# State times w_in in 64x32 TensorE tiles, state reads in column pairs, another split of the vector work, and another order of the first loads

## The chip, the cores and the metric

The kernel runs on one core of one Trainium2 chip. A core has TensorE (PE) for matmuls, VectorE (DVE), ScalarE (ACT) and GpSimd (POOL) for elementwise work, and SyncE (SP), which here only issues DMAs. The metric is the device time of one execution in microseconds, lower is better. The kernel before takes 754.55 us (median of three runs, 753.77 to 754.71).

## What is computed

```python
def _attn_ref(x, state):                       # x 4x8x512x64, state 4x8x32x64
    scores = scale * np.matmul(x, state.transpose(0, 1, 3, 2))
    ...
    xread = np.matmul(a, state)                # a: softmax over the 32 states
    scores2 = scale * np.matmul(state, x.transpose(0, 1, 3, 2))
    ...
    sread = np.matmul(a2, x)                   # a2: softmax over the 512 tokens
    return np.concatenate([xread, sread], axis=2)

def _moe_ref(x, w_in, w_out):                  # 2304 tokens, 512 -> 2048 -> 512
    h = x @ w_in
    g = np.where(h >= 1, h, np.where(h <= -1, 0.0, (h + 1) ** 2 / 4))
    return g @ w_out

def _moe2_ref(x, w_a, w_b, w_out):             # 512 -> 1536 -> 512
    return ((x @ w_a) * (x @ w_b)) @ w_out
```

Attention between 512 tokens and 32 state slots per head (32 heads, 64 wide) gives 2304 rows of 512 numbers, which then pass through two feed-forward blocks. The weights arrive as 8-byte floats and are converted on the chip.

## The kernel before

**The stages.** Phase one, up to the first matmul of 368 columns, does the attention and the first product `h = x @ w_in` with its gate. The rest (`b_chunk`, `ab_run`, `o_run`) does the other three products, by Strassen-like sums of seven, each product in three matmuls of high and low halves; the change leaves it as it is.

**Phase one.** Heads are taken four at a time, in eight "quads" `k`; two quads make one batch of 512 tokens. The tokens' rows of `h` don't need `xread` itself: since `xread = a @ state`, `h` is the sum over heads of `a @ (state @ w_in)`. So `w_state` multiplies the states by the rows of `w_in` that belong to their heads (plain f32, 64 head dimensions contracted, 32 slots a head), for one batch and one group `n` of four of the sixteen 128-wide blocks `f` of `w_in`; the result leaves its bank as a high half (ACT, `hi_of`) and a low half (DVE). `h_mm(j, f)` then multiplies it by the attention weights `att` of batch `j` (six matmuls of 512 columns), 64 such units in all. `a_qk` makes the scores, `a_soft` the softmax over slots and `att`, `s_soft` the softmax over tokens, `s_tr` transposes it on PE, `s_read` multiplies it by the tokens, and `h_state` makes the `h` rows of the states from that (128 matmul records). The blocks of `w_in` and, later, of `w_out` (`vraw`) are converted by `conv`: a DMA into a staging slot, a byte copy (L389 on DVE for `w_in`, on ACT for the others), an ACT copy that rounds (L321), and a DVE operation that puts the word together (L395). Before, `w_state` runs per quad: two matmuls of 64 weight columns with 128 rows, of which half are zeros, side by side in the array.

**The gate** of a unit, four PSUM banks in turn: ACT reads the bank (L613), ACT or POOL squares (L620, L622), DVE combines it with the bank (L627) and so frees it; the result is stored to DRAM (`g_d`). There are 68 gates: 16 for each batch `j` of tokens, and four for the state rows (after the 48th).

**The order.** `Flow` records each operation with the engines that may run it, a cost and its dependencies, and `order()` places them one by one; that fixes each engine's instruction list and, where a choice of engines was given, the engine. An engine runs its list strictly in order. All DMAs are issued by SP, in order, and an issue waits for what was in its slot.

Of the kernel before, what the change touches and what calls it, by code (L numbers as in the profile page):

```python
# [19 lines left out]
class Flow:  # L20
# [48 lines left out]
    def order(self):  # L69
# [24 lines left out]
        for i in range(n - 1, -1, -1):  # L94
# [70 lines left out]
def attention_then_two_mlps(  # L165
# [31 lines left out]
    STEPS = (0, 5, 10, 16, 22, 28, 34, 40)  # L197

# [102 lines left out]
    def t_ts(n):  # L301
        return 0.16 + n * 0.00052
# [55 lines left out]
    def conv(src, k, stage, z, dst=None, by="ACT"):  # L358
# [27 lines left out]
        if by == "ACT":  # L386
            act(to, of, n, AF.Copy, regs(place), regs(z), saturate=False)
        else:
            op({"DVE": t_tt(n)}, lambda e: nc.vector.tensor_copy(to(U8), of(U8)), regs(place), regs(z))  # L389
        act(to, z, n, AF.Copy, regs(z), regs(z), saturate=False)  # L390
# [27 lines left out]
    stage_a = Ring([V("F0", 8256 * i, 2050) for i in range(2)])  # L418
    z_a = Ring([V("F0", 16512 + 4096 * i, 1024) for i in range(1)])
# [9 lines left out]
    def w_in(f, k):  # L429
        conv(w1_k[0, f : f + k], k, stage_a(), z_a(), win.sub(512 * f, 512 * k), by="DVE")  # L430

    def aset(i):
# [9 lines left out]
        {**sets[k % 2], "st": V("FS", 32768 + 1024 * (k % 4), 256), "sm": V("FS", 69632 + 256 * (k % 4), 64)}  # L442
# [9 lines left out]
    def st_load(b):  # L452
        v = V("FS", 32768 + 2048 * (b % 2), 512)
# [3 lines left out]
                out=v().rearrange("p (k n) -> p k n", k=2), in_=st_d[2 * b : 2 * b + 2].rearrange("k p n -> p k n")  # L457
# [3 lines left out]
            1 << 18,  # L461
# [8 lines left out]
    def a_qk(k):  # L470
# [19 lines left out]
    def a_soft(k):  # L490
# [22 lines left out]
        split(*att[k], d["at"])  # L513

    def w_state(b, q, n):
        d = qs[2 * b + q]
        ab = abank()

        def emit(e):
            for p in range(2):  # L520
                r = slice(64 * p, 64 * p + 64)
                c = (2 * q + p) * P
                w = win()[:, 2048 * n : 2048 * (n + 1)].rearrange("p (f x) -> p f x", x=512)[:, :, c : c + P]
                nc.tensor.matmul(  # L524
                    banks[ab][r, :].rearrange("p (f x) -> p f x", x=P), d["st"]()[:, r], w, start=True, stop=True
                )

        op({"PE": 1.05}, emit, regs(d["st"], win.sub(2048 * n, 2048)), [bank(ab)])
        hi, lo = wsum[n][q]
        src = lambda: banks[ab]  # L530
        hi_of(hi, src, 512, [bank(ab)], regs(hi))
        tt(lo, src, lambda: hi(F32), ALU.subtract, 512, [bank(ab)] + regs(hi), regs(lo))

    def s_soft(k):
# [45 lines left out]
    def s_read(k):  # L580
# [756 lines left out]
```

## Time and profile before

| | us |
|---|---|
| median of three runs | 754.55 |
| the profiled execution | 753.63 |
| its span, first to last instruction | 751.9 |
| PE busy | 721.4 |
| DVE busy | 562.6 |
| ACT busy | 433.2 |
| POOL busy | 76.4 |

The profile takes one execution apart. Busy time is the union of an engine's instructions; the rest is waiting. PE is nearly always busy after 62 us, so the others' totals say little by themselves: what counts is, stage by stage, whether PE waits, and for what. The time outside the span is 1.73 us in the profiled execution.

### The profile page before, as it was taken

What the parts mean: (1) busy time and instruction counts of PE and PEld (TensorE: products, weight loads), DVE (VectorE), ACT (ScalarE), POOL (GpSimd) and SP (SyncE); (2) the same over time, 40 slices, a digit from 0 to 9 for tenths busy, and PEclk for the clock granted to TensorE, in tenths of its full rate; (3) what the DMA queues carried; (4) which work ended last, traced back from release to release, by engine and by line L of the source; (5) the groups of instructions that cost most, each with busy time, mean ns of one, the idle gap of its engine ahead of it and who ended that gap; (6) DMA issues with size and microseconds to landing.
All of it is one profiled execution on the core that took longest, in us unless ns stands there. A gap on an engine that the chain in (4) does not pass through costs nothing.

```text
span 751.9 us, 11651 instructions
## 1 busy us (share of the span) xinstructions
PE 721.4 (96%) x4454; PEld 663.6 (88%) x4454; DVE 562.6 (75%) x790; ACT 433.2 (58%) x656; POOL 76.4 (10%) x67
## 2 busy tenths in 40 slices
PE   4898999998999999999999999999999999999997
PEld 2455676685899999999999999999999999999997
DVE  5798887848889668789999966566645699977660
ACT  2687899848644444566556766555433455544440
POOL 2223464318100000000000000000000000000000
PEclk7899999999999999999999999999999999999999
DMA  9776777427756514626134666546452249444211
GB/s 335 252 266 213 256 259 267 168 93 247 253 189 189 169 41 148 208 69 193 63 118 146 209 238 211 188 137 221 136 168 79 83 129 292 135 141 127 86 43 43
DMA packets 75513, 127.92 MB, mean 170 GB/s; under 512 B 5696, under 2 KB 50240, under 8 KB 75456
## 3 DMA queue, kind: packets, MB, share of 16 engines
q1 hardware_dynamic: 75456, 127.16, 51.4%
q8 instruction: 35, 0.57, 0.3%
q14 instruction: 22, 0.18, 0.1%
HBM read 83.89 MB, written 43.25 MB: 169 GB/s over the span
## 4 chain that ended last, share of the span: by engine, by line
PE 81%; DMA 6%; DVE 6%; ACT 2%; POOL 2%; issue 2%; SPq 0%; DVEq 0%; ACTq 0%; POOLq 0%
PE bank L345 74%; DMA f<-in_w_dram 3%; PE bank L524 2%; PE bank L658 2%; ACT f L321 2%; POOL f L622 1%; DMA fs<-in_st_dram 1%; PE bank L478 1%; DVE r L330 1%; DMA p_d<-f 1%; DVE f L627 1%; PE bank L589 1%; DMA f<-p_d 1%; DVE rh L330 1%; DVE fs L395 1%
## 5 line engine op out<-in xcount | busy, mean ns | idle before, releaser
L345 PE MATMUL bank<-rh,r 128*128 128x352 f32 (+2 forms) x1398 | 222.2, 316 | 2.1 <-DVE f L330 0.9
L345 PEld LDWEIGHTS bank<-rh,r 128*128 128x128 f32 x1398 | 215.7, 189 | 3.0 <-DVE f L330 1.2
L321 ACT ACTIVATE f<-bank 128x368 f32<-128x368 f32 (+3 forms) x183 | 82.8, 455 | 142.1 <-PE bank L345 141.7
L345 PE MATMUL bank<-r,r 128*128 128x368 f32 (+1 forms) x960 | 157.5, 316 | 0.0
L345 PEld LDWEIGHTS bank<-r,r 128*128 128x128 f32 x960 | 148.7, 189 | 0.5 <-DVE r L330 0.5
L321 ACT ACTIVATE rh<-f 128x736 fp32r<-128x736 f32 (+5 forms) x120 | 100.7, 845 | 78.9 <-PE bank L345 69.5
L330 DVE TENSOR_TENSOR rh<-f,rh 128x736 fp32r<-128x736 f32 (+5 forms) x120 | 116.1, 972 | 36.3 <-ACT rh L321 33.6
L330 DVE TENSOR_TENSOR f<-bank,f 128x368 f32<-128x368 f32 (+2 forms) x168 | 85.4, 516 | 76.1 <-PE bank L345 65.9
L345 PE MATMUL bank<-r 128*128 128x512 f32 (+1 forms) x582 | 123.1, 363 | 4.1 <-DVE f L627 4.0
L345 PEld LDWEIGHTS bank<-r 128*128 128x128 f32 x582 | 95.0, 191 | 34.0 <-DVE f L627 7.9
L330 DVE TENSOR_TENSOR f<-f 128x256 f32<-128x256 f32 (+7 forms) x142 | 116.8, 842 | 2.9 <-DMA f<-p_d 2.4
L330 DVE TENSOR_TENSOR r<-f,r 128x768 fp32r<-128x768 f32 (+5 forms) x88 | 94.3, 1079 | 18.1 <-ACT r L321 17.7
L321 ACT ACTIVATE r<-f 128x768 fp32r<-128x768 f32 (+5 forms) x88 | 80.7, 924 | 32.2 <-PE bank L345 22.9
L321 ACT ACTIVATE f<-f 128x1024 fp8e5<-128x1024 f32 (+1 forms) x77 | 85.6, 1111 | 17.7 <-DVE f L395 6.3
L345 PE MATMUL bank<-rh 128*128 128x352 f32 (+2 forms) x564 | 93.1, 318 | 0.0
L345 PEld LDWEIGHTS bank<-rh 128*128 128x128 f32 x564 | 88.4, 189 | 0.6 <-DVE f L330 0.6
L345 PE MATMUL bank<-r,rh 128*128 128x368 f32 (+1 forms) x480 | 81.0, 316 | 0.0
L345 PEld LDWEIGHTS bank<-r,rh 128*128 128x128 f32 x480 | 74.7, 189 | 0.2 <-DVE rh L330 0.2
L524 PE MATMUL bank<-fs 128*64 128x512 f32 x128 | 33.1, 632 | 14.5 <-DVE fs L395 12.2
L622 POOL TENSOR_TENSOR f<-f 128x512 f32<-128x512 f32 x25 | 34.1, 1376 | 61.6 <-ACT f L613 61.5
L395 DVE SCALAR_TENSOR_TENSOR f<-f 128x1024 uint32<-128x1024 uint32 (+1 forms) x34 | 33.1, 973 | 6.0 <-ACT f L321 5.9
L627 DVE SCALAR_TENSOR_TENSOR f<-f,bank 128x512 f32<-128x512 f32 x40 | 26.8, 678 | 13.0 <-ACT f L620 6.7
(50 smaller groups left out, 376.7 us busy)
## 6 DMA issues: line engine op xcount, KB each, us to landing
f<-in_w_dram SPq DMA_DIRECT2D x25, 1024.0 KB, 5.4
f<-p_d SPq DMA_DIRECT2D x17, 768.0 KB, 5.3
f<-g_d SPq DMA_DIRECT2D x32, 368.0 KB, 4.6
g_d<-f SPq DMA_DIRECT2D x40, 256.0 KB, 2.7
f<-in_w_dram SPq DMA_DIRECT2D x18, 512.0 KB, 3.9
p_d<-f SPq DMA_DIRECT2D x48, 184.0 KB, 2.1
g_d<-fs SPq DMA_DIRECT2D x28, 256.0 KB, 2.6
f<-g_d SPq DMA_DIRECT2D x16, 352.0 KB, 3.8
```

Of the source, the lines that this page charges most:

```text
L321: lambda e: nc.scalar.activation(dst(), src(), func, **{k: (v() if callable(v) else v) for k, v in kws.items()}),
L330: op({"DVE": t_tt(n)}, lambda e: nc.vector.tensor_tensor(dst(), a(), b(), alu), rd, wr)
L345: nc.tensor.matmul(o, w, x, start=first and k == 0, stop=last and k == n - 1, skip_group_check=onto)
L395: lambda e: nc.vector.scalar_tensor_tensor(out(U32), words_of(1, U32)(), 5, z(U32), ALU.logical_shift_right, ALU.bitwise_or),
L478: nc.tensor.matmul(banks[b][r, :], d["st"]()[:, r], d["xld"]()[:, p * 512 : (p + 1) * 512], start=True, stop=True)
L524: nc.tensor.matmul(banks[ab][r, :].rearrange("p (f x) -> p f x", x=P), d["st"]()[:, r], w, start=True, stop=True)
L589: nc.tensor.matmul(banks[ab][:, p * 64 : (p + 1) * 64], d["xn"]()[:, c * 256 + p * 128 : c * 256 + (p + 1) * 128], d["a2t"]()[:, c * 128 + ...
L622: nc.gpsimd.tensor_tensor(g(), g(), g(), ALU.mult)
L627: lambda e: nc.vector.scalar_tensor_tensor(g(), g(), 1.0, h(), ALU.min, ALU.max),
L658: nc.tensor.matmul(banks[b][:, P * i : P * i + P], w[:, P * c : P * c + P], xs()[:, P * c : P * c + P], start=c == 0, stop=c == 3,)
```

## The change

`w_state` takes both quads of a batch in one operation: eight matmuls of 64 rows by 32 weight columns in place of four of 128 by 64. The zero padding is gone, so the loads of the states halve. The placement alternates: head `j` of quad `q` reads partitions `64*(j%2)`, and writes partitions `32*(j ^ q)` of the bank of its quad. `a_qk` is done in the same kind of tile (four matmuls in one bank). `s_read` uses 16 matmuls of 64 weight columns and 32 moving columns in place of 8 of 128 and 64, and its result leaves in one ACT copy instead of two. In `conv`, the byte copy may go to DVE or POOL (`w_in`) or ACT or POOL (`vraw`); the low half of `att`, the Strassen sums of `vraw` may go to POOL too, and the square of a gate to DVE. `w_in` gets five staging slots and two scratch buffers instead of two and one. The first loads are the tokens of quads 0 and 1, then the states, then five blocks of `w_in`; the token loads for `s_read` of quads 0 and 1 wait for the planner's first `w_state`. `s_tr` and `s_read` come some units after `s_soft`.

```diff
-    def conv(src, k, stage, z, dst=None, by="ACT"):
+    def conv(src, k, stage, z, dst=None, by=("ACT",)):
...
+        t = 0.18 + 0.00116 * n
+        op({x: {"A": t, "D": t_ts(n), "P": 0.2 + 0.0014 * n}[x[0]] for x in by}, copy, regs(place), regs(z))
...
+    stage_w = Ring([V("F0", o, 2050) for o in (0, 8256, 28160, 36416, 44672)])
+    z_w = Ring([V("F0", o, 1024) for o in (16512, 52928)])
...
-        conv(w1_k[0, f : f + k], k, stage_a(), z_a(), win.sub(512 * f, 512 * k), by="DVE")
+        conv(w1_k[0, f : f + k], k, stage_w(), z_w(), win.sub(512 * f, 512 * k), by=("DVE", "POOL") if f else ("DVE", "ACT"))
...
-            for p in range(2):
-                r = slice(64 * p, 64 * p + 64)
+            for j in range(4):
+                r, o, x = slice(64 * (j % 2), 64 * (j % 2) + 64), NS * (j ^ (k % 2)), 512 * (j // 2)
                 nc.tensor.matmul(
-                    banks[b][r, :], d["st"]()[:, r], d["xld"]()[:, p * 512 : (p + 1) * 512], start=True, stop=True
+                    banks[b][o : o + NS, :],
+                    d["st"]()[r, NS * j : NS * j + NS],
+                    d["xld"]()[r, x : x + 512],
...
-        split(*att[k], d["at"])
...
+        op(
+            {"DVE": t_tt(512), "POOL": 1.3},
+            lambda e: eng(e).tensor_tensor(lo(), d["at"](), hi(F32), ALU.subtract),
...
+    def w_state(b, n, f0=0, f1=4):
+        st = [qs[2 * b + q]["st"] for q in range(2)]
+        ab = [abank() for _ in range(2)]
...
+            for j in range(4):
+                for q in range(2):
+                    h, c, o = j % 2, 2 * q + j // 2, NS * (j ^ q)
+                    w = win()[64 * h : 64 * h + 64, 2048 * n + 512 * f0 : 2048 * n + 512 * f1]
+                    nc.tensor.matmul(
+                        banks[ab[q]][o : o + NS, :cols].rearrange("p (f x) -> p f x", x=P),
+                        st[q]()[64 * h : 64 * h + 64, NS * j : NS * j + NS],
+                        w.rearrange("p (f x) -> p f x", x=512)[:, :, c * P : c * P + P],
...
+        flow.gate = first_w[0] if k < 2 else None
         load(d["xn"], lambda: xn_d[k], (), 1 << 19)
...
+                    for e2 in range(2):
+                        nc.tensor.matmul(
+                            banks[ab][64 * e2 : 64 * e2 + 64, p * NS : (p + 1) * NS],
+                            d["xn"]()[:, c * 256 + p * 128 + e2 * 64 : c * 256 + p * 128 + (e2 + 1) * 64],
...
-        op({"ACT": t_act(512), "POOL": 1.1}, square, regs(g), regs(g))
+        op({"ACT": t_act(512), "DVE": t_tt(512), "POOL": 1.3}, square, regs(g), regs(g))
...
-    def v_sum(dst, a, b, alu):
-        tt(dst, a, b, alu, words(dst), regs(a, b), regs(dst))
+    def v_sum(dst, a, b, alu, engs=("DVE",)):
...
+        st_load(0)
         a_load(0)
-        st_load(0)
+        flow.rush = 8.0
         a_load(1)
-        w_in(0, 1)
-        w_in(1, 1)
+        flow.rush = 0.0
+        w_in(0, 2)
         warm(WARM)
         a_part(0)
+        a_part(1)
         w_in(2, 2)
-        w_part(0, 0)
-        a_part(1)
-        w_part(0, 1)
+        first_w.append(len(flow.ops))
+        w_state(0, 0, 0, 2)
+        w_state(0, 0, 2, 4)
```

On SP, from the first issue on, the loads stand like this before (`in_xt` and `in_xn` are the tokens in two layouts, `in_st` the states, `in_w` the weights; 128x4096 is one block of `w_in`, 128x2x4096 two):

```order
L369 DMA f_66<-in_w_dram 128x4096 x2
L309 DMA fs<-in_xt_dram 128x512 x2
L456 DMA fs<-in_st_dram 128x2x256
L309 DMA fs<-in_xt_dram 128x512 x2
L309 DMA fs<-in_xn_dram 128x1024
L456 DMA fs<-in_st_dram 128x2x256
L309 DMA fs<-in_xn_dram 128x1024
L369 DMA f_66<-in_w_dram 128x2x4096 x2
L309 DMA fs<-in_xt_dram 128x512 x4
```

and like this now:

```order
L314 DMA fs<-in_xt_dram 128x512 x4
L468 DMA fs<-in_st_dram 128x2x128
L374 DMA f_66<-in_w_dram 128x2x4096 x5
L468 DMA fs<-in_st_dram 128x2x128
L314 DMA fs<-in_xt_dram 128x512 x4
L374 DMA f_66<-in_w_dram 128x2x4096
L314 DMA fs<-in_xn_dram 128x1024 x2
L374 DMA f_66<-in_w_dram 128x2x4096 x2
```

The tokens and states of the first two quads have moved ahead of all weights, five double blocks of `w_in` follow without a gap, and the `in_xn` loads stand behind six of the eight.

On POOL, the list after the first two quads' softmax was this before (L498 and L508 are `a_soft`, L622 squares of gates):

```order
L498 TENSOR_TENSOR fs<-fs 128x512 x2
L508 TENSOR_TENSOR fs<-fs 128x512 x2
L622 TENSOR_TENSOR f_66<-f_66 128x512 x2
L498 TENSOR_TENSOR fs<-fs 128x512 x2
L622 TENSOR_TENSOR fs<-fs 128x512 x2
L508 TENSOR_TENSOR fs<-fs 128x512 x2
```

and is this now (L514 and L524 are `a_soft`, L396 byte copies of `conv`, L533 low halves of `att`, L651 squares):

```order
L514 TENSOR_TENSOR fs<-fs 128x512 x2
L524 TENSOR_TENSOR fs<-fs 128x512 x2
L396 COPY f_66<-f_66 128x1024
L533 TENSOR_TENSOR r_65<-fs,r_65 128x512 x2
L396 COPY f_66<-f_66 128x1024
L651 TENSOR_TENSOR f_66<-f_66 128x512 x2
L651 TENSOR_TENSOR fs<-fs 128x512 x3
L396 COPY f_66<-f_66 128x1024
```

Byte copies and low halves stand between the softmax steps and the squares now; over the whole program POOL has nine byte copies, four low halves and five sums of 128x4x256 that it didn't have, and three squares fewer (42 for 45).

## Rows read from the trace of the kernel before

**Rows 1.** Busy time by stage: stretch, length, engines' busy us, granted clock, DMA share, GB/s.
```profile
0.00:78.10 78.10, 59.60 (x268) 35.05 (x269) 60.06 (x112) 50.02 (x84) 23.11 (x26) 0.89 0.76 269
78.10:156.30 78.20, 75.91 (x379) 51.96 (x378) 63.46 (x94) 68.96 (x107) 34.45 (x28) 1.00 0.66 226
156.30:198.30 42.00, 37.90 (x211) 31.14 (x211) 27.62 (x32) 27.49 (x38) 18.75 (x13) 0.96 0.64 213
198.30:751.90 553.60, 547.95 (x3601) 545.46 (x3600) 411.42 (x555) 286.74 (x428) 0.05 (x1) 1.00 0.45 145
```

**Rows 2.** PE's waits, longest in total first: total us, times, longest us.
```profile
PE bank L524 <- DVE fs L395: 12.2, 4, 9.3
...
PE bank L345 <- DVE f L627: 4.0, 3, 3.4
```

**Rows 3.** PE in order of time: start us, us, records; idle time before in brackets.
```profile
21.94 3.46 PE L524 MATMUL bank<-fs 128*64 128x512 f32 x8 [9.28 <-DVE fs L395]
...
26.18 3.06 PE L345 MATMUL bank<-r 128*128 128x512 f32 x12
...
75.88 1.94 PE L524 MATMUL bank<-fs 128*64 128x512 f32 x8
...
82.56 1.08 PE L478 MATMUL bank<-fs 128*64 128x512 f32 x4
83.57 2.00 PE L589 MATMUL bank<-fs 128*128 128x64 f32 x16
...
198.34 8.21 PE L345 MATMUL bank<-rh,r 128*128 128x368 f32 x48
```

**Rows 4.** DVE in order of time: the 16th and the 48th gate.
```profile
77.45 0.65 DVE L627 SCALAR_TENSOR_TENSOR f<-f,bank 128x512 f32<-128x512 f32 x1
...
155.62 0.67 DVE L627 SCALAR_TENSOR_TENSOR fs<-fs,bank 128x512 f32<-128x512 f32 x1
```

**Rows 5.** Groups by line and shape in 0 to 198.3 us: busy us, mean ns.
```profile
L622 POOL TENSOR_TENSOR f<-f 128x512 f32<-128x512 f32 x25 | 34.1, 1376 | 61.6 <-ACT f L613 61.5
...
L589 PEld LDWEIGHTS bank<-fs 128*128 128x128 f32 x128 | 15.2, 191 | 3.8 <-ACT fs L321 2.7 <-ACT fs L547 0.8
...
L321 ACT ACTIVATE f<-f 128x1024 fp8e5<-128x1024 fp8e5 x8 | 11.0, 1373 | 0.9 <-DMA f<-in_w_dram 0.9
...
L330 DVE TENSOR_TENSOR f<-f 128x1024 f32<-128x1024 f32 x8 | 10.0, 1252 | 0.0
...
L620 ACT ACTIVATE f<-f 128x512 f32<-128x512 f32 x14 | 8.8, 628 | 0.3
...
L524 PEld LDWEIGHTS bank<-fs 128*64 128x64 f32 x128 | 7.8, 140 | 31.8 <-DVE fs L395 15.0 <-issue 10.1 <-ACT fs L321 4.9
L330 DVE TENSOR_TENSOR r<-fs,r 128x512 fp32r<-128x512 f32 x8 | 6.6, 826 | 0.0
...
L389 DVE COPY f<-f 128x1024 uint8<-128x1024 uint8 x7 | 5.3, 756 | 2.5 <-DMA f<-in_w_dram 2.5
```

**Rows 6.** Busy time by stretch: the head, and the state rows' product.
```profile
0.00:9.00 9.00, 4.26 (x24) 4.10 (x24) 3.27 (x6) 2.82 (x3) 0.70 (x6) 0.94 0.77 257
...
155.00:169.00 14.00, 14.00 (x128) 14.00 (x127) 4.56 (x7) 4.24 (x7) 0.00 (x0) 1.00 0.29 96
```

**Rows 7.** The first scores on PE, in order of time.
```profile
8.97 3.68 PE L478 MATMUL bank<-fs 128*64 128x512 f32 x8 [3.38 <-DMA fs<-in_st_dram]
```

**Rows 8.** A piece of the chain that ended last: start us, us, what.
```profile
46.94 7.80 DMA f<-in_w_dram
```

**Rows 9.** DVE in order of time: the same operation twice.
```profile
110.15 2.05 DVE L330 TENSOR_TENSOR r<-f,r 128x1024 fp32r<-128x1024 f32 x1
...
125.55 1.21 DVE L330 TENSOR_TENSOR r<-f,r 128x1024 fp32r<-128x1024 f32 x1
```

**Rows 10.** POOL in order of time: two products of 512 columns.
```profile
102.41 1.04 POOL L622 TENSOR_TENSOR fs<-fs 128x512 f32<-128x512 f32 x1 [1.54 <-ACT fs L613]
...
111.08 2.02 POOL L508 TENSOR_TENSOR fs<-fs 128x512 f32<-128x512 f32 x1
```

More of the change, by code (lines that the diff above doesn't have):

```diff
@@ L101, in order @@
                 late[i] = min(late[i], ideal[i])
+        late = [x - self.hurry[i] for i, x in enumerate(late)]
         free = dict.fromkeys(self.LAT, 0.0)
@@ L385, in conv, with copy @@
         to, of = lambda dt=F8: byte(z, 4)(dt)[:, :, 3], lambda dt=F8: byte(place.sub(2, 2 * n), 8)(dt)[:, :, 0]
[L386 to L390, printed above, removed]
+        def copy(e):
+            if e == "ACT":
+                nc.scalar.activation(to(), of(), AF.Copy, saturate=False)
+            else:
+                eng(e).tensor_copy(to(U8), of(U8))
+        t = 0.18 + 0.00116 * n
+        op({x: {"A": t, "D": t_ts(n), "P": 0.2 + 0.0014 * n}[x[0]] for x in by}, copy, regs(place), regs(z))
+        act(to, z, n, AF.Copy, regs(z), regs(z), t=t, saturate=False)
         out = words_of(1) if dst is None else dst
@@ L460, in st_load @@
             regs(v),
-            1 << 18,
+            1 << 17,
         )
@@ L512, in a_soft @@
         op({"DVE": 0.71}, lambda e: nc.vector.transpose(d["at"](), t1()), regs(t1), regs(d["at"]))
-        split(*att[k], d["at"])
-    def w_state(b, q, n):
-        d = qs[2 * b + q]
-        ab = abank()
-        def emit(e):
[L520 to L532, printed above, removed]
+        hi, lo = att[k]
@@ new lines, in a_soft @@
+        hi_of(hi, d["at"], 512, regs(d["at"]), regs(hi))
+        op(
+            {"DVE": t_tt(512), "POOL": 1.3},
+            lambda e: eng(e).tensor_tensor(lo(), d["at"](), hi(F32), ALU.subtract),
+            regs(d["at"], hi),
+            regs(lo),
+        )
+    def w_state(b, n, f0=0, f1=4):
+        st = [qs[2 * b + q]["st"] for q in range(2)]
+        ab = [abank() for _ in range(2)]
+        cols = P * (f1 - f0)
+        def emit(e):
+            for j in range(4):
[6 more added lines that the diff above has]
+                        w.rearrange("p (f x) -> p f x", x=512)[:, :, c * P : c * P + P],
+                        start=True,
+                        stop=True,
+                    )
+        op({"PE": 0.3 + cols * 0.0018}, emit, regs(*st, win.sub(2048 * n + 512 * f0, 512 * (f1 - f0))), [bank(b) for b in ab])
+        for q in range(2):
+            hi, lo = (v.sub(P * f0, cols) for v in wsum[n][q])
+            src = lambda q=q: banks[ab[q]][:, :cols]
+            hi_of(hi, src, cols, [bank(ab[q])], regs(hi))
+            tt(lo, src, lambda hi=hi: hi(F32), ALU.subtract, cols, [bank(ab[q])] + regs(hi), regs(lo))
@@ L565, in s_soft @@
         )
+        flow.gate = first_w[0] if k < 2 else None
         load(d["xn"], lambda: xn_d[k], (), 1 << 19)
+        flow.gate = None
     def s_tr(k):
@@ L648, in h_mm @@
         g = (qring if 16 * j + f < SWITCH else qlast)()
-        gate(b, g, lambda: store(lambda: g_d[f, :, S * j : S * j + S], g, [dram("G", f, S * j, S * j + S)], 1 << 18))
+        here = [dram("G", f, S * j, S * j + S)]
+        gate(b, g, lambda: store(lambda: g_d[f, :, S * j : S * j + S], g, here, 1 << 18))
     def h_state(n):
@@ L727, in v_split @@
         tt(rows(lo), src, rows(hi, F32), ALU.subtract, n, regs(src, hi), regs(lo))
-    def v_sum(dst, a, b, alu):
-        tt(dst, a, b, alu, words(dst), regs(a, b), regs(dst))
+    def v_sum(dst, a, b, alu, engs=("DVE",)):
+        n = words(dst)
+        op(
+            {x: t_tt(n) if x == "DVE" else 0.2 + 0.0021 * n for x in engs},
+            lambda e: eng(e).tensor_tensor(dst(), a(), b(), alu),
+            regs(a, b),
+            regs(dst),
+        )
     parts = ((0, 4), (4, 8))
+    BOTH = ("DVE", "POOL")
     def v_early():
@@ L1129, in phase_one @@
     def phase_one():
-        zero(z_a())
+        for _ in range(2):
+            zero(z_w())
         def a_part(k):
@@ L1167, in phase_one @@
                 s_soft(k)
-                s_tr(k)
-                s_read(k)
                 if k + 2 < NQ:
@@ L1174, in phase_one @@
                     a_part(k + 2)
+            if t in READS:
+                k = READS.index(t)
+                s_tr(k)
+                s_read(k)
             if 12 <= t < 44 and t % 4 == 0:
                 flow.gate = units[-1]
-                conv(w1_k[1, nv : nv + 2], 2, stage_a(), z_a(), V("F0", vraw[nv].at, 1024))
+                conv(w1_k[1, nv : nv + 2], 2, stage_a(), z_a(), V("F0", vraw[nv].at, 1024), ("ACT", "POOL"))
                 flow.gate = None
```

52 lines of the change are left out of this document (24 added, 28 removed).

## The prediction

> **What bounds the kernel now.** I first read the busy time stretch by stretch [rows 1], cut at events that the changed kernel has too: the end of the 16th gate on DVE (78.10 us), of the 48th (156.30) [rows 4], and the first matmul of 368 columns (198.34) [rows 3]. Call the stages A, B and C; the last 553.6 us lie behind them. There PE is busy 547.95 of 553.6 us and the change adds no matmul, so I leave that part as it is. In B PE is busy 75.91 of 78.2 us (97%), ACT 68.96 (88%), DVE 63.46 (81%), POOL only 34.45 (44%): PE sets the pace, ACT is close behind, POOL has room. In A PE is busy 59.60 of 78.1, DVE 60.06, ACT 50.02, so no engine fills it. The list of waits says why [rows 2]: `w_state` waited 12.2 us for the converted `w_in`, 9.28 of them before its first matmul at 21.94 us [rows 3]. A later load still stands on the last chain, issued at 46.94 us and 7.8 us long [rows 8]. C has 4.1 us without PE work; gates that DVE took late cost 4.0 in all, nearly all of it there [rows 2].
>
> **PE's work.** One `w_state` for a batch and a group was two pairs of matmuls, 1.94 us for eight records [rows 3]. It is now eight smaller matmuls, sixteen records. No row has a tile of 64 rows by 32 columns. If all eight run at once, the price is that of one pair, 1.94/2 = 0.97 us; if they find no more room than before, 1.94. I take 1.2: `s_read`'s records, 64 moving columns behind a load of 128 weight columns, follow each other at 2.00/16 = 0.125 us [rows 3], a quarter of that for 32 columns is 0.03, and eight more records make 0.97 + 0.24. Sixteen such steps exist, eight in B: 8 x 0.74 = 5.9 us less there.
>
> `s_read` goes from 16 records to 32, with half the weight columns. A load of 64 columns is 191 - 140 = 51 ns shorter than one of 128 [rows 5]. One after another the 32 cost 32 x 0.0625 = 2.0 us, no gain; two columns of the array at once, 1.0. I take 1.3, somewhat under the middle, since the two matmuls of a pair now write separate columns of the array, as `w_state`'s pairs do, whose four records of 512 columns take 0.97. Five of the eight are in B: 5 x 0.7 = 3.5 us. `a_qk` had two tiles at once and has four; I leave it at 1.08.
>
> So PE in B: 75.91 - 5.9 - 3.5 = 66.5 us.
>
> **DVE and ACT in B**, by counting both lists between the 16th and the 48th gate. DVE loses five sums (1.25 each [rows 5]), two low halves of `att` (0.83), two splits of 1024 (1.5, between the two of rows 9) and one word operation (about 1.25), and gets five squares (about 0.63, half a sum) and one more `a_soft` and `s_soft` share that slides over from A (about 4): -6.3 - 1.7 - 3.0 - 1.2 + 3.1 + 4.0 = -5.1, so 58.4 us. ACT loses eight byte copies (1.37), three squares (0.63), two splits (about 1.05), gets some 2 of softmax: 68.96 - 11.0 - 1.9 - 2.1 + 2.0 = 56.0. POOL takes what left: of the nine copies, four low halves and five sums most fall here. A copy on POOL has no row: 0.76 if it runs as on DVE [rows 5], 2.75 if it costs two products of 512 (1.38 each, the mean); I take 1.6. A sum is two products, 2.1 by the short row to 4.0 by the long one [rows 10]; I take 2.75. POOL goes to about 58 us.
>
> PE stays the longest. At the same 97% B takes 68.5 us. With POOL at over 80% squares wait longer in its queue, and behind each the gate on DVE and the bank that PE needs; I add 2. **B: 70.5, 7.7 us less.** Ends: 66.6 (PE without a gap, 1.0 a step) and 74.
>
> **Stage A.** The first scores waited for the states until 8.97 us [rows 7], queued behind 1.57 MB; now they stand behind 1.05. At the head's 257 GB/s [rows 6] that is 2.0 us. The first `w_state` needs one double block instead of two single and one double, and its staging slot waits for nothing. That block ends 2.2 MB into the queue, 8.6 us, and the states landed 1.8 us behind such a count (1.83 MB, 7.1 us): 10.4. Then come on ACT and DVE a byte copy 1.37, a softmax step 0.63, a second copy 1.37 and the word, about 1.25 (a sum of the same size) [rows 5], together 4.6, and a us for what stands between them: the first `w_state` at 16 us instead of 21.94, the first unit, behind the high and low halves, near 21.5 instead of 26.18. The last block of `w_in` stands 11.3 MB into the queue; if the DMA engines don't rest, 269/0.76 = 354 GB/s [rows 1], it lands at 34 us instead of 54.7 [rows 8], so loads leave the chain.
>
> What is left is DVE. Its list up to the 16th gate loses three copies of 1024 and two of 512 (3.2 us), two low halves (1.7), two softmax steps and a half that slide into B (about 4), and gets a memset (0.9) and a square (0.6): 60.06 - 7.4, say 53. Before, DVE was busy 3.27 us until 9.0 [rows 6] and 56.8 of the 69.1 us after, 82%. Now 51 us of work (53 less the memsets) begin at 7. At 82% the gate comes at 69, at 95% at 61. I take 67, nearer to the first, because the chain copy, ACT, word, product, high half, low half still passes between engines for each group. PE has about 40 us of work from 16 on and fits. **A: 67, 11.1 us less.** Ends: 61 and 71.
>
> **Stage C.** DVE gets two splits and one word from B and four squares, about 6.7 us, ACT about 4. During the state rows' product DVE and ACT are busy only 4.56 and 4.24 of 14 us [rows 6], and that hides them; without this cover they would cost up to 6. Of the five sums on POOL two or three now stand before squares. **C: 42.5, 0.5 more.** Ends: 40 (the late gates vanish) and 45.
>
> Sum: 753.63 - 11.1 - 7.7 + 0.5 = 735.3 for an execution like the profiled one; the median of the runs lies 0.92 above that, so **736**.
>
> **Shared paths.** POOL and DVE get in each other's way already: the same split took DVE 2.05 us beside POOL work and 1.21 without [rows 9], a product took POOL 2.02 in the same microseconds and 1.04 alone [rows 10]. In B, two-input DVE work on SBUF falls from about 26 to 18 us while POOL's rises from 34 to 58, so the product of the two, the chance to meet, stays about the same; I add nothing beyond the 2 us above. The Trainium skill (SBUF — State Buffer, on the engine side of the ports) says that a DVE operation with two SBUF inputs and a GpSimd operation exclude each other for a whole instruction. The rows agree; by that rule every move to GpSimd is paid partly by DVE, which is the second rival below.
>
> **Rivals.**
> *Slower: halves that share a bank take turns.* In `a_qk` all four tiles write one bank, from alternating halves of the rows; in `w_state` each bank gets tiles from both halves in turn. If two row halves can't write one bank at once, matmuls run strictly in order and `w_state` becomes four steps of 0.97 = 3.9 us, `a_qk` four of about 1.0. B: 66.5 + 8 x 2.7 + 2 x 2.9 = 93.9, at 97% 97 us, 18.6 slower than before; A has eight more such steps and six `a_qk`, 39 us on top of 40, and ends near 89, 11 slower. Total about 784. It turns at a step price of about 2.3 us. Against it: outputs of one bank lie on different partitions, and the `j ^ q` puts the two halves that share a column on different banks. No row has two row halves. The Trainium skill (TensorEngine Tiling (Array Packing), Gotcha 1) says that different row tiles cannot access the same PSUM bank at the same time; read strictly, that is this rival, and no run here shows it yet.
> *POOL in the way.* If copies and sums on POOL cost their upper ends and collide with DVE, gates come late throughout: A 70, B 75, C 45, total 754.6 - 8.1 - 3.2 + 3 = 746. For it: POOL would be the engine with the second longest busy time in B. Against: the squares have a second and a third engine.
> *PE alone decides.* If 1.0 us a step holds and A is as tight as B: A 62, B 67, C 41.5, total 754.6 - 16.1 - 11.2 - 0.5 = 727.
> *`s_read` gains nothing*, its 32 loads one after another: 3.5 us back in B and 1.4 in A, total 741. In the forecast's range.
>
> **How the numbers follow.** Forecast (731 to 741): 0.52. PE alone (723 to 731): 0.16. POOL in the way (741 to 750): 0.22. Row halves taking turns: 0.06. Between 750 and 756: 0.04. Predicted is the forecast, 736. The range leaves out the slow rival and the tail of the fast one: 726 to 749. A measurement of this kernel tells 0.2% (1.5 us) from no change; faster 0.91, same 0.03, slower 0.06.
>
> **What would show it.** `w_state`'s 16 records in 1.0 to 1.4 us, `s_read`'s 32 in 1.0 to 1.6; the first `w_state` near 16 us; the 16th gate near 67, the 48th near 137.5, the first 368-column matmul near 180; no gap over 4 us after that that wasn't there. Wrong if a step takes over 1.9 us, if PE waits in B for more than 4 us, or if the stages are as told and the time is not.

## The result, and the profile after

The changed kernel takes **731.91 us** (median of four runs, 731.11 to 733.22; the kernel before on the same chip 754.63): ratio **0.9703**, 95% interval 0.9686 to 0.9720. The profiled execution has a span of 729.3 us where the one of before has 751.9. The forecast was 736.0, with a range of 726 to 749.

The span by stages, cut as in [rows 1] at the ends of the 16th and the 48th gate and at the first 368-column matmul (columns: stretch, length, busy us and instructions of PE, PEld, DVE, ACT, POOL, granted clock, DMA share, GB/s):

```profile
0.00:67.50 67.50, 52.29 (x424) 31.14 (x425) 56.84 (x98) 46.25 (x76) 35.61 (x33) 0.90 0.84 293
67.50:136.10 68.60, 68.60 (x559) 48.32 (x558) 63.78 (x100) 58.39 (x96) 45.42 (x36) 1.00 0.80 268
136.10:175.60 39.50, 34.10 (x180) 27.73 (x179) 37.69 (x38) 28.23 (x39) 24.31 (x14) 0.96 0.63 211
175.60:729.30 553.70, 548.04 (x3601) 545.51 (x3600) 412.75 (x555) 287.70 (x428) 0.00 (x0) 1.00 0.45 146
```

All of the gain lies before the first 368-column matmul; the rest takes 553.7 us as it did before. Stage A is 10.6 us shorter, B 9.6, C 2.5. In B PE has no idle time left. PE in order of time (start us, us, what, number of records, idle time before in brackets):

```profile
7.51 1.09 PE L490 MATMUL bank<-fs 64*32 64x512 f32 x16 [1.86 <-DMA fs<-in_st_dram]
16.06 1.11 PE L548 MATMUL bank<-fs 64*32 64x256 f32 x16 [7.46 <-DVE fs L405]
...
21.71 5.00 PE L350 MATMUL bank<-r 128*128 128x512 f32 x12
...
65.20 1.09 PE L548 MATMUL bank<-fs 64*32 64x512 f32 x16
66.22 5.75 PE L350 MATMUL bank<-r 128*128 128x512 f32 x24
...
72.79 1.06 PE L490 MATMUL bank<-fs 64*32 64x512 f32 x8
73.77 1.66 PE L350 MATMUL bank<-r 128*128 128x512 f32 x6
...
77.19 1.13 PE L621 MATMUL bank<-fs 128*64 128x32 f32 x32
78.25 1.65 PE L350 MATMUL bank<-r 128*128 128x512 f32 x6
...
130.79 14.56 PE L688 MATMUL bank<-fs 128*128 128x128 f32 x128
...
153.96 10.07 PE L350 MATMUL bank<-r 128*128 128x512 f32 x36 [2.19 <-DVE f L656]
166.70 7.12 PE L350 MATMUL bank<-r 128*128 128x512 f32 x30 [2.68 <-DVE f L656]
...
175.58 1.25 PE L350 MATMUL bank<-rh,r 128*128 128x368 f32 x6
```

Against [rows 3]: sixteen records of `w_state` (L548, once L524) follow each other to the next matmul in 66.22 - 65.20 = 1.02 us, where the same work, both quads of a batch, took 1.94 in eight records of larger tiles; `s_read` (L621, once L589) has 1.06 for 2.00; `a_qk` (L490) has 0.98 to the next matmul for 1.01. The first `w_state` comes at 16.06 for 21.94, the first unit at 21.71 for 26.18. The waits of PE, against [rows 2] (total us, times, longest us):

```profile
PE bank L548 <- DVE fs L405: 7.5, 1, 7.5
PE bank L350 <- DVE f L656: 5.7, 5, 2.7
PE bank L548 <- DVE r L335: 3.2, 1, 3.2
```

The wait for converted weights has shrunk from 12.2 us in four pieces to one of 7.5 and one of 3.2 for the low half behind it. The wait for late gates (L656, once L627) has grown from 4.0 to 5.7, and nearly all of it is in C.

**A better cut.** The 48th gate no longer marks what it did. DVE in order of time around it (start us, us, what):

```profile
130.70 2.20 DVE L405 SCALAR_TENSOR_TENSOR f<-f 128x1024 uint32<-128x1024 uint32 x1
132.82 2.06 DVE L335 TENSOR_TENSOR r<-f,r 128x1024 fp32r<-128x1024 f32 x1
134.81 0.68 DVE L335 TENSOR_TENSOR r<-bank,r 128x512 fp32r<-128x512 f32 x1
135.41 0.67 DVE L656 SCALAR_TENSOR_TENSOR fs<-fs,bank 128x512 f32<-128x512 f32 x1
```

The gate at 135.41 stood behind two operations on weights for later; PE had begun the state rows' product at 130.79 and did not miss the bank. So below, B ends where `h_state` starts on PE (154.57 before, 130.79 after), and C runs from there to the first 368 columns:

| us | A | B, to `h_state` | C |
|---|---|---|---|
| before | 78.1 | 76.5 | 43.8 |
| after | 67.5 | 63.3 | 44.8 |

By this cut C has grown by a us. Its two lines, before and after:

```profile
154.57:198.34 43.77, 39.67 (x226) 32.87 (x225) 29.39 (x34) 28.09 (x39) 18.84 (x14) 0.96 0.65 217
```

```profile
130.79:175.58 44.79, 39.39 (x232) 33.02 (x225) 42.98 (x42) 31.99 (x43) 27.32 (x16) 0.96 0.59 200
```

DVE is busy 42.98 of 44.79 us there (96%), 13.6 more than before, and POOL 27.32 instead of 18.84. Stage C thus became the question of the experiments, beside what each part of the change is worth.

### The profile page after: what moved, and what is told of

Its sections match the earlier page's. It is cut to its first block, busy times and chain, and to the rows that moved or that the text cites. A ratio compares the mean times of both kernels' runs of the same rounds, so it can differ in the third digit from the quotient of the medians.

```text
span 729.3 us, 12250 instructions
## 1 busy us (share of the span) xinstructions
PE 703.0 (96%) x4758; PEld 652.7 (89%) x4758; DVE 571.1 (78%) x788; ACT 420.6 (58%) x637; POOL 105.3 (14%) x82
## 5 line engine op out<-in xcount | busy, mean ns | idle before, releaser
L335 DVE TENSOR_TENSOR f<-bank,f 128x368 f32<-128x368 f32 (+2 forms) x168 | 85.5, 517 | 76.5 <-PE bank L350 69.0
L350 PE MATMUL bank<-r 128*128 128x512 f32 (+1 forms) x582 | 125.8, 367 | 5.4 <-DVE f L656 5.4
L335 DVE TENSOR_TENSOR r<-f,r 128x768 fp32r<-128x768 f32 (+5 forms) x88 | 97.8, 1118 | 20.1 <-ACT r L326 19.9
L763 DVE TENSOR_TENSOR f<-f 128x256 f32<-128x256 f32 (+5 forms) x119 | 90.7, 782 | 1.0 <-DMA f<-p_d 0.6
L326 ACT ACTIVATE f<-f 128x1024 fp8e5<-128x1024 f32 (+1 forms) x42 | 47.9, 1142 | 2.9 <-POOL f L396 2.3
L405 DVE SCALAR_TENSOR_TENSOR f<-f 128x1024 uint32<-128x1024 uint32 (+1 forms) x34 | 35.0, 1030 | 2.6 <-ACT f L326 2.4
L394 ACT ACTIVATE f<-f 128x512 fp8e5<-128x512 fp8e5 (+1 forms) x29 | 30.6, 1055 | 11.1 <-DVE f L405 6.9
L642 ACT ACTIVATE f<-bank,half 128x512 f32<-128x512 f32 x40 | 26.9, 685 | 14.1 <-PE bank L350 11.5
L548 PE MATMUL bank<-fs 64*32 64x512 f32 (+1 forms) x272 | 20.9, 604 | 10.6 <-DVE fs L405 7.5
```

The source lines that it names most:

```text
L326: lambda e: nc.scalar.activation(dst(), src(), func, **{k: (v() if callable(v) else v) for k, v in kws.items()}),
L335: op({"DVE": t_tt(n)}, lambda e: nc.vector.tensor_tensor(dst(), a(), b(), alu), rd, wr)
L350: nc.tensor.matmul(o, w, x, start=first and k == 0, stop=last and k == n - 1, skip_group_check=onto)
L394: nc.scalar.activation(to(), of(), AF.Copy, saturate=False)
L405: lambda e: nc.vector.scalar_tensor_tensor(out(U32), words_of(1, U32)(), 5, z(U32), ALU.logical_shift_right, ALU.bitwise_or),
L548: nc.tensor.matmul(banks[ab[q]][o : o + NS, :cols].rearrange("p (f x) -> p f x", x=P), st[q]()[64 * h : 64 * h + 64, NS * j : NS * j + NS] ...
```

## The experiments

Times are compared by ratios to the kernel before on the same chip; the column us is 754.6 times (ratio - 1).

| kernel | ratio (95%) | us | A | B | C |
|---|---|---|---|---|---|
| after | 0.9703 (0.9686 to 0.9720) | -22.4 | 67.5 | 63.3 | 44.8 |
| u_place | 0.9865 (0.9839 to 0.9891) | -10.2 | 72.2 | 71.0 | 45.7 |
| u_sread | 0.9877 (0.9847 to 0.9908) | -9.3 | 71.2 | 74.9 | 44.3 |
| p_sread | 0.9761 (0.9729 to 0.9793) | -18.0 | 68.8 | 66.2 | 46.0 |
| u_load | 0.9865 (0.9823 to 0.9906) | -10.2 | 79.6 | 68.0 | 44.5 |
| u_pool | 0.9721 (0.9695 to 0.9746) | -21.1 | 67.5 | 63.9 | 46.4 |
| b_tiles | 0.9787 (0.9763 to 0.9811) | -16.1 | 74.4 | 63.5 | 45.6 |
| b_load | 0.9994 (0.9972 to 1.0017) | -0.5 | 82.2 | 72.3 | 43.7 |
| v_c | 0.9646 (0.9619 to 0.9673) | -26.7 | 69.9 | 63.2 | 41.0 |
| v_sum | 0.9711 (0.9691 to 0.9732) | -21.8 | 68.3 | 63.3 | 45.4 |
| v_pc | 0.9655 (0.9637 to 0.9672) | -26.0 | 68.2 | 64.3 | 40.6 |
| b_sq | 0.9947 (0.9921 to 0.9973) | -4.0 | 75.9 | 75.6 | 39.3 |

Two things hold for all. Where an edit changes a cost or a choice of engines, `order()` lays every list out anew, so a difference between two rows is that of two plans. And A, B and C are read from the one profiled execution of each kernel, while the ratio uses all of them: b_sq and the kernel before run the same lists up to the 48th unit, and still differ by 3.1 us in A and B (PE's granted clock in the first 25 us was 0.80 in the one and 0.66 in the other). A difference of two or three us in a single cell says little. The profiled execution of u_load is its slowest (747.65 us, median 742.88), that of b_load too (754.72 and 752.2), and that of b_sq its fastest (746.3 and 748.47).

### The placement of the tiles: u_place

```diff
-                r, o, x = slice(64 * (j % 2), 64 * (j % 2) + 64), NS * (j ^ (k % 2)), 512 * (j // 2)
+                r, o, x = slice(64 * (j % 2), 64 * (j % 2) + 64), NS * j, 512 * (j // 2)
...
-                    h, c, o = j % 2, 2 * q + j // 2, NS * (j ^ q)
+                    h, c, o = j % 2, 2 * q + j // 2, NS * j
```

(and the same in `s_read`). Every list of instructions stays as it is; only the two quads' tiles now fall on the same four of the eight places of the array.

> The changed kernel with the same lists on every engine, but w_state's two quads write the same partitions (j instead of j ^ q, and the same for the scores and the state reads, so the result stays the same): the two tiles of a pair now share their place in the array. Theory (PE sets the pace of stage B, and the gain of w_state is that all eight tiles run at once): a step goes from 1.02 us to between 1.9 and 4.3, the whole to 742 to 780 us, with PE the engine without gaps in B. Rival (DVE and ACT set B, PE's step is covered): a step is longer too, but the time stays within 3 us of 731.9.

Measured: 743.69 us, at the low end of what was expected. Two steps of PE:

```profile
69.86 1.94 PE L548 MATMUL bank<-fs 64*32 64x512 f32 x16
77.39 1.94 PE L548 MATMUL bank<-fs 64*32 64x512 f32 x16
```

A step takes 1.94 us, the price of before, and B is 7.7 us longer for its eight steps (8 x 0.92 = 7.4). So here two tiles on the same place ran one after the other, tiles on different places at once, and `j ^ q` alone carries about 12 of the 22 us.

### The state reads: u_sread and p_sread

Both give `s_read` back its 8 matmuls of 128 weight columns. u_sread also gives the planner the old cost (1.9) and two copies, so all lists are new; p_sread keeps the planner's costs, so that the lists stay those of the changed kernel, with both copies issued in the place of one.

```diff
-                    for e2 in range(2):
-                        nc.tensor.matmul(
-                            banks[ab][64 * e2 : 64 * e2 + 64, p * NS : (p + 1) * NS],
...
+                    nc.tensor.matmul(
+                        banks[ab][:, p * 64 : (p + 1) * 64],
+                        d["xn"]()[:, c * 256 + p * 128 : c * 256 + (p + 1) * 128],
...
-        op({"PE": 1.1}, emit, regs(d["xn"], d["a2t"]), [bank(ab)], loose=True)
+        op({"PE": 1.9}, emit, regs(d["xn"], d["a2t"]), [bank(ab)], loose=True)
```

> The changed kernel with the state reads as before: 8 matmuls of 128 weight and 64 moving columns, two ACT copies. Theory: a read goes from 1.06 back to about 1.95 us, 5 of 8 lie in stage B where PE has no gaps, so 4 to 6 us slower, 736 to 738. Rival (they fall into gaps or DVE is the bound): within 1.5 us of 731.9.

> As u_sread, but the planner is told the price of the new reads and one copy, so every list stands as in the changed kernel, with 8 matmuls and two copies in the place of 16 and one. Theory (a read's own price is 0.85 us on PE, and u_sread's 13 us came mostly of lists laid out anew): 735 to 739. Rival (the reads themselves cost that much, by waits behind them): 742 to 746.

Measured: u_sread 745.0 us, 7 over its range; p_sread 736.01, within it. PE around one read in u_sread:

```profile
93.92 2.00 PE L620 MATMUL bank<-fs 128*128 128x64 f32 x16 [1.79 <-ACT fs L326]
95.85 1.47 PE L548 MATMUL bank<-fs 64*32 64x512 f32 x2
97.70 1.96 PE L548 MATMUL bank<-fs 64*32 64x512 f32 x14 [0.38 <-ACT fs L326]
99.59 7.40 PE L350 MATMUL bank<-r 128*128 128x512 f32 x24
```

Here the new list sends PE into a read whose ACT copy isn't ready, and the matmuls after the wait are slow: 24 records in 7.40 us where the changed kernel has 5.75 for as many at 66.22. In p_sread, with the lists kept, the reads cost 1.89 each (1.06 in the changed kernel), with no such wait in B, and the kernel is 4.4 us slower by the ratios. That is the reads' own price; the other 9 us of u_sread are the plan.

### The three parts by themselves: u_load, u_pool, b_tiles, b_load

u_load is the changed kernel with the first loads, slots and opening order of before. u_pool is the changed kernel with the engine choices of before. b_tiles is both: only tiles and reads are changed. b_load is the kernel before with the new loads, five slots, two scratch buffers and the opening order alone. u_load's edit, and u_pool's:

```diff
-    stage_w = Ring([V("F0", o, 2050) for o in (0, 8256, 28160, 36416, 44672)])
-    z_w = Ring([V("F0", o, 1024) for o in (16512, 52928)])
+    stage_w = Ring([V("F0", o, 2050) for o in (0, 8256)])
+    z_w = Ring([V("F0", o, 1024) for o in (16512,)])
...
-        flow.gate = first_w[0] if k < 2 else None
...
```

```diff
-        conv(w1_k[0, f : f + k], k, stage_w(), z_w(), win.sub(512 * f, 512 * k), by=("DVE", "POOL") if f else ("DVE", "ACT"))
+        conv(w1_k[0, f : f + k], k, stage_w(), z_w(), win.sub(512 * f, 512 * k), by=("DVE",))
...
-            {"DVE": t_tt(512), "POOL": 1.3},
+            {"DVE": t_tt(512)},
...
-        op({"ACT": t_act(512), "DVE": t_tt(512), "POOL": 1.3}, square, regs(g), regs(g))
+        op({"ACT": t_act(512), "POOL": 1.1}, square, regs(g), regs(g))
...
-    BOTH = ("DVE", "POOL")
+    BOTH = ("DVE",)
...
```

(What the last cut leaves out is the opening order in u_load, and the byte copy of `vraw`, on ACT alone, in u_pool.)

> The changed kernel with the first loads, staging slots and first steps as before (single blocks of w_in first, two slots, one scratch buffer, in_xn early). Theory: the first w_state comes 4 to 6 us later, the last block of w_in near 50 us instead of 34, stage A 5 to 9 us longer, B and C unchanged: 737 to 741. Rival (A is DVE's work alone, loads are covered): within 2 us of 731.9.

> The changed kernel with the engine choices of before (byte copies on DVE for w_in and ACT for the rest, low halves of att and the sums on DVE, squares on ACT or POOL); tiles and loads as changed. Theory: ACT gets 11 us back in stage B (54.7 to about 67, more than B's 63.5) and DVE 5 in A, so A and B together 6 to 10 us longer; stage C, where DVE and POOL block each other now, 2 to 4 shorter; in all 735 to 740. Rival (collisions of DVE and POOL eat what the move gives): 732 or faster.

> The kernel before with the tiles alone: w_state for both quads, scores and reads in the new tiles, reads some units later; first loads, staging and engine choices as before. Theory (stage A is held by the loads, stage B by PE): the 16th gate stays near 78 us, the state rows' product starts 8 to 10 us sooner, 743 to 747. Rival (the tiles are worth all that u_place and u_sread lost, 25 us): 730 or less.

> The kernel before with the first loads, the five staging slots and the two scratch buffers alone. Theory: the 16th gate comes near 69 us, stage B stays 78 (PE 97% busy with the old steps), 743 to 747. Rival (without the shorter steps PE and DVE fill stage A too and the loads give nothing): 751 to 755.

Measured: u_load 742.88, u_pool 732.81, b_tiles 737.53, b_load 752.2 us. Only u_load is near what the theory said (2 us above its range, with B longer too); the other three missed, and b_load came out where its rival had it.

**Tiles alone** give 16.1 of the 22.4 us. Their B, 63.5 us, is that of the whole change: neither the loads nor POOL matter there. **The loads alone** give nothing, though they do what they should: the first unit starts at 21.83 us instead of 26.18. Two stretches of b_load, and then the same two of before (columns as above):

```profile
20.00:40.00 20.00, 14.74 (x54) 7.95 (x50) 17.98 (x31) 15.09 (x24) 2.15 (x2) 0.67 0.95 372
...
40.00:154.50 114.50, 114.47 (x547) 75.43 (x545) 92.00 (x149) 96.43 (x156) 51.01 (x44) 0.98 0.60 209
```

```profile
20.00:40.00 20.00, 17.45 (x76) 8.92 (x76) 15.37 (x28) 14.09 (x25) 4.10 (x4) 0.87 0.74 260
...
40.00:154.50 114.50, 108.35 (x526) 71.32 (x524) 94.69 (x154) 98.20 (x157) 48.46 (x41) 1.00 0.67 229
```

From 40 us on PE never rests in b_load and yet `h_state` starts at 154.47, as before (154.57). It had fallen behind until then: between 20 and 40 us it did 54 records where 76 were done before, since it waited again (2.17 and 3.09 us) and the granted clock was lower (0.67, 0.87 before). Up to 154.5 us PE is idle 4.4 us less and busy 4.4 us more (138.15 for 133.71) with the same matmuls. So in this execution the idle time that the loads saved came back as slower matmuls, and from 40 us on, with the old, dearer tiles, PE had no idle time left to give. On top of the tiles the loads are worth something: b_tiles to u_pool -5.0 us, all of it in A (74.4 to 67.5).

**The POOL moves** are worth 1.3 us on top of that (u_pool to the change, 0.9 us by medians), which the intervals do not separate from nothing. A is 67.5 with and without them. Nor did they relieve DVE there: it is busy 56.84 us with them and 56.44 without, in part because the four byte copies that stayed on DVE took 1.23 us each, while all eight took 0.81 in u_pool. In C u_pool is not better than the change (46.4 for 44.8 us); PE there:

```profile
167.27 8.44 PE L350 MATMUL bank<-r 128*128 128x512 f32 x30 [5.43 <-DVE f L656]
```

So the moves did not make C tight; it is tight without them. Why u_load, which has tiles and POOL moves on the old loads, is slower than b_tiles, which has the tiles alone (742.9 and 737.5), is not settled: its A is 5.2 us longer and its B 4.5, but in an execution 4.8 us above its median, and two replanned lists differ in too much.

### The last stage: v_c, v_sum, v_pc, b_sq

v_c takes the sums of `vraw` off POOL, and the squares of the units from the 49th on off POOL and DVE, so that ACT does them. v_sum does the first alone. v_pc is u_pool with squares of those units on ACT alone. b_sq is the kernel before with the same: its lists are those of before up to the 48th unit, and PE's is the same throughout.

```diff
-    def gate(b, g, put):
+    def gate(b, g, put, late=False):
...
-        op({"ACT": t_act(512), "DVE": t_tt(512), "POOL": 1.3}, square, regs(g), regs(g))
+        op({"ACT": t_act(512)} if late else {"ACT": t_act(512), "DVE": t_tt(512), "POOL": 1.3}, square, regs(g), regs(g))
...
-    BOTH = ("DVE", "POOL")
+    BOTH = ("DVE",)
```

(`late` is true from unit 48 on, counted from 0; the last two lines alone are v_sum, the others alone, on u_pool and on the kernel before, v_pc and b_sq.)

> The changed kernel with POOL left out of stage C: the sums only on DVE, the squares of the last 16 units only on ACT. Theory (DVE is 96% busy in C because its operations with two SBUF inputs and POOL's block each other, 2.0 us for splits that take 1.2 alone, and PE waits 5.4 us for gates that DVE is late with): C shorter by 3 to 5, 727 to 730. Rival (DVE has too much work of its own there, or ACT gets late): 731 to 735.

> The changed kernel, only that the Strassen sums of w_out (L763) run on DVE alone, as before the change; squares, low halves and byte copies keep their three and two engines. PE's list is the same as in the changed kernel; DVE gets five sums more, POOL five fewer. Theory (it is the long sums on POOL that slow DVE's instructions of two SBUF inputs in the last stage): DVE loses about 5 x 1.25 us of room but its splits and sums go back from 2.0-2.4 to 1.25 us, gates come sooner, and the time is 727 to 729.5, like the run without sums and squares on POOL (726.8). Rival (the squares on POOL were what hurt there): 731 to 734, no gain. It turns at about 730.

> The changed kernel with the engine choices of before throughout (byte copies of w_in on DVE, low halves and sums on DVE, no squares on DVE), and, from the 48th unit on, squares on ACT alone. So POOL has nothing of the change's work and nothing in the last stage. The same choices with squares allowed on POOL took 732.8. Theory (POOL work in the last stage is what costs there, whatever else is chosen): 727 to 730, the same gain of some 4 us. Rival (the gain of 726.8 needs DVE relieved by POOL in the first two stages, so that it enters the last one without arrears): 731 to 735.

> The kernel before, only that the squares of the units from the 49th on run on ACT alone (POOL has one left in the last stage of phase one). PE's list is the same, and every list is the same up to the 48th unit. Theory (squares on POOL in the last stage cost before the change too: they come late and slow DVE's two-input work, so the 4.0 us that PE waited for gates goes): 749.5 to 752, the gain of about 3 us being independent of the change. Rival (the last stage is tight only in the changed kernel, which brings more DVE work into it): 752.5 to 755, no gain.

Measured: v_c **726.76**, v_sum 731.96, v_pc **727.65**, b_sq 748.47 us. v_pc lies in its theory's range, v_c just under it. v_sum says that moving the sums alone gains nothing: the time is that of the change. Half of its theory held, for a split on DVE is back at 1.38 us from 1.98 and a sum at 1.49 from 2.38 (other splits of 1024 columns took 1.64 for 1.32), but DVE has five sums more to do and stays full (43.87 of 45.44 us). v_pc says the gain does not need POOL's help in A and B. b_sq says that it was there to be had before the change (4.0 us, interval 2.0 to 6.0, somewhat over what was expected). So it is taking the squares off POOL that pays, and v_c and v_pc beat both kernels. In all three runs that show it the sums are on DVE; the squares off POOL with the sums left on it was not run. (Of b_sq only C counts, for the scatter told above.) C in v_sum, v_c, v_pc and b_sq, one line each:

```profile
131.56:177.00 45.44, 39.10 (x232) 32.98 (x225) 43.87 (x46) 31.30 (x41) 20.83 (x14) 0.96 0.60 201
```

```profile
133.09:174.05 40.96, 37.59 (x232) 32.03 (x225) 35.83 (x41) 32.34 (x49) 6.00 (x4) 1.00 0.64 220
```

```profile
132.46:173.02 40.56, 37.71 (x231) 32.05 (x225) 36.63 (x43) 34.60 (x53) 4.10 (x3) 1.00 0.62 212
```

```profile
151.49:190.82 39.33, 36.94 (x226) 32.19 (x225) 23.45 (x32) 28.39 (x46) 1.09 (x2) 1.00 0.65 224
```

Each column tells a piece. POOL is nearly empty in the last three. DVE in b_sq has two instructions fewer than before (32 for 34) and is busy 23.45 us instead of 29.39. About half of that is other work in the stretch (three operations of 1024 columns fewer, one of 736 more), about half shorter instructions: a split of 736 columns takes 0.92 us for 1.28. The same groups in C of before and of b_sq (line, shape, count, busy us, mean ns):

```profile
L622 POOL TENSOR_TENSOR f<-f 128x512 f32<-128x512 f32 x13 | 18.8, 1466 | 24.9 <-ACT f L613 24.9
...
L330 DVE TENSOR_TENSOR r<-f,r 128x1024 fp32r<-128x1024 f32 x2 | 3.3, 1638 | 0.0
```

```profile
L620 ACT ACTIVATE f<-f 128x512 f32<-128x512 f32 x16 | 9.6, 634 | 0.1
...
L330 DVE TENSOR_TENSOR r<-f,r 128x1024 fp32r<-128x1024 f32 x1 | 1.2, 1218 | 0.0
```

A square took POOL 1.47 us beside DVE's work and takes ACT 0.63, and the gate on DVE that waits for it can free PE's bank that much sooner. Whether the late square or DVE's slower splits hold the gate is not separated: in the chain of work that ended last in the kernel before, four squares on POOL stand from 171.46 to 177.94 us, and then, right before PE's longest wait ends, three splits on DVE of 2.52 (two) and 1.98 us. And PE is *busy* 2.7 us less in b_sq than before with the same matmuls (36.94 for 39.67), at a granted clock of 1.00 instead of 0.96. PE behind `h_state` in before, and in b_sq:

```profile
168.89 15.11 PE L345 MATMUL bank<-r 128*128 128x512 f32 x60
187.43 1.75 PE L345 MATMUL bank<-r 128*128 128x512 f32 x6 [3.43 <-DVE f L627]
189.41 7.09 PE L345 MATMUL bank<-r 128*128 128x512 f32 x24 [0.23 <-DVE f L627]
```

```profile
165.80 14.00 PE L345 MATMUL bank<-r 128*128 128x512 f32 x60
181.01 7.14 PE L345 MATMUL bank<-r 128*128 128x512 f32 x30 [1.20 <-DVE f L627]
```

The 30 records behind the long wait take 8.84 us (1.75 + 7.09) for 7.14. What happens there is plainer in u_pool, whose wait is longer; the next two lines are that wait and the time right behind it:

```profile
161.80:167.30 5.50, 0.07 (x2) 0.04 (x1) 5.50 (x5) 2.88 (x4) 3.72 (x3) 0.95 0.86 290
167.30:170.00 2.70, 2.70 (x7) 2.12 (x8) 2.70 (x4) 0.00 (x0) 0.00 (x0) 0.50 0.73 269
```

After 5.4 us in which PE stood, the clock granted is 0.50 for the next 2.7 us, its lower level of 1.2 GHz. Here a late gate was paid twice: as the wait, and as the slow matmuls behind it. Of the 4.4 us that b_sq's C is shorter, 1.7 are idle time and 1.7 the matmuls behind the long wait, where the kernel before had a granted clock of 0.77 and then 0.72 from 187.43 to 194.0 us. About 1 us more is in the 60 records before the wait (15.11 for 14.00 us), at a granted clock of 1.00 in both; its cause is not shown.

## Why the prediction was right, and where not

**PE's work: right, and a little better than taken.** `w_state` was taken at 1.2 us between 0.97 and 1.94; it is 1.02, the low end. `s_read` was taken at 1.3 between 1.0 and 2.0; it is 1.06. `a_qk` was left at 1.08 and measured 1.06. u_place and p_sread show that these are the causes: by the ratios, 12.2 us are gone with the step back at 1.94, and 4.4 with the reads back at 1.89.

**Stage B: mechanism right, one term too many.** 66.5 us of work at 97%, plus 2 for squares waiting on POOL, gave 70.5; by the gates it is 68.6. That this is so near is partly luck of the cut: the 48th gate ends 5.3 us after `h_state` began (1.7 before). Up to `h_state`, before and after (columns as above):

```profile
78.10:154.57 76.47, 74.18 (x364) 50.23 (x362) 61.73 (x92) 68.36 (x106) 34.40 (x28) 1.00 0.65 225
```

```profile
67.50:130.79 63.29, 63.29 (x512) 43.01 (x510) 58.47 (x96) 54.63 (x91) 42.41 (x35) 1.00 0.84 281
```

PE's work fell by 10.9 us, where 9.4 was forecast, and the 2.3 us of idle time went too: PE never had to wait for a bank. By this cut B is 13.2 us shorter, where 7.7 was forecast. The 3% and the 2 us are the mis-sized term, with 1.5 us of PE's work.

**Stage A: right by its steps, with luck in the last one.** First `w_state` 16 us (16.06), first unit 21.5 (21.71), the 16th gate 67 (67.5). For that gate DVE was to do 51 us of work from 7 us on, at 85%; it did 54.95, at 91%, and the two errors cancel. What it credits is only half shown: the loads alone bring the first unit forward as well, and gain nothing (b_load); tiles and loads together make the 10.6 us. That POOL would relieve DVE in A was wrong: without the moves the gate is at 67.5 too, and DVE's work is the same (u_pool).

**Stage C: the size right, the ground wrong.** 42.5 was forecast (+0.5); by the gates 39.5 (-2.5), by PE's milestones +1.0. The step that failed is "that hides them": DVE was to get 6.7 us more and got 10.1 by the gates, 13.6 by PE's milestones, and has no room left (95 and 96%). By the milestones some of what is missing is work that moved in, two more splits and a second word; most are collisions, operations of DVE and POOL that lengthen each other, which the prediction set at nothing. In C after the change (the same columns as above):

```profile
L763 POOL TENSOR_TENSOR f<-f 128x1024 f32<-128x1024 f32 x5 | 13.2, 2649 | 6.1 <-DVE rh L335 3.7 <-DVE r L335 1.2 <-DVE f L763 1.2
...
L335 DVE TENSOR_TENSOR r<-f,r 128x1024 fp32r<-128x1024 f32 x6 | 11.8, 1984 | 0.0
...
L763 DVE TENSOR_TENSOR f<-f 128x1024 f32<-128x1024 f32 x2 | 4.8, 2380 | 0.0
```

A split is 1.98 us on the mean against 1.21 alone [rows 9], a sum on DVE 2.38 against 1.25 [rows 5]: six splits and two sums cost 6.9 us more than alone, where two splits of 1.64 and three sums of 1.32 cost 1.1 in the same stretch before. With the sums off POOL (v_sum) a split is back at 1.38. The product of busy times was the wrong measure, since it was taken for B, and the long sums meet DVE's longest work in C. This is the rule of the Trainium skill (SBUF — State Buffer, on the two separate sides) that the prediction kept for its second rival: a DVE operation with two SBUF inputs and a GpSimd operation that reads SBUF can block each other for a whole instruction. The rows agree, in that both get longer.

**POOL's prices: right; its place wrong.** A byte copy was taken at 1.6 us (mean 1.59 over nine: 1.85 in A, 1.38 from A's end to the 48th gate), a sum at 2.75 (2.65). But POOL in B is 45.4 us, not 58: four of nine copies fall into A, and four of five sums behind the 48th gate.

**The rivals.** *Row halves take turns* is out: at 72.79 four tiles of `a_qk`, two from each half of the rows, write one bank, and 0.98 us later the next matmul starts, as with the two tiles of before (82.56 to 83.57, [rows 3]). The rule of the Trainium skill (TensorEngine Tiling (Array Packing), Gotcha 1) that would have made the kernel slower did not show here; the row decides. *POOL in the way* was right on C's collisions, and right that they spread: in A the byte copies on DVE take 1.23 us for 0.76, in B the words 1.53 for 1.24 and the two splits 2.01 for 1.50. It was wrong on what they cost there, for in B PE does not wait at all. Its core, that work on POOL holds up gates, is what v_c and v_pc took out for 4 to 5 us. *PE alone decides* (727) described B, and not A, where PE still stands 15 of 67.5 us. *`s_read` gains nothing* is out.

**The sum.** Against the forecast A is 0.5 us longer, B 1.9 and C 3.0 shorter (cut at the gates): 735.3 - 4.4 = 730.9, and with the 0.92 between execution and median 731.8, where 731.9 was measured. That is bookkeeping and no further proof. Of C's 3.0 a part is only the cut, since the 48th gate came late at no cost to PE: cut at PE's milestones A is 0.5 longer than forecast, B 5.5 shorter and C 0.5 longer, so the whole miss is B's waits and work that were put too high.

## What to carry to other kernels

Small f32 tiles paid here because all eight 64x32 places of the array were filled with different tiles; look at where each falls, since two on one place ran one after the other. Before giving elementwise work to GpSimd, look at whose instruction waits for its result and what VectorE does in the same microseconds: the copies moved to POOL left VectorE as busy as it was, and squares on POOL in front of the last gates cost about 4 us here, in both kernels, and on ACT they did not. The new load order gained nothing with the old tiles, and 5 us with the new ones, which left PE room to use what came early.

## What the runs showed of the hardware

- Four 64x32 tiles from both halves of the rows write one bank at full rate (8 records, 0.98 us to the next matmul), and eight on two banks as well (16 records, 1.02); eight matmuls on four places take 1.94.
- After PE stood for 5.4 us, the granted clock was 0.50 for the next 2.7 us, and 30 matmuls of 512 columns took 8.44 instead of 7.12 us. It isn't so after each wait: in the changed kernel 30 take 7.12 right behind a wait of 2.68 us, at a granted clock of 1.00, while 36 take 10.07 behind one of 2.19, at 0.67 in their first 2.64 us.
- A square of 128x512 took POOL 1.47 us in the mean beside DVE's work (1.04 in [rows 10]), and ACT 0.63.
- Four byte copies of 128x1024 on DVE took 1.23 us each in stage A, where POOL did four others (1.85 us each); all eight on DVE took 0.81 (u_pool).
